# The beginning of a lightning-attention and feed-forward kernel put in another order: planner lengths, half groups of tokens, filler transposes

## The chip, the core and the metric

The kernel runs on one core of a Trainium2 chip. Such a core has a matrix engine (TensorE, here PE, with its weight loads shown as PEld), VectorE (DVE), ScalarE (ACT), GpSimd (POOL) and SyncE (SP), which here only issues transfers. The engines run side by side, each takes its own instructions strictly in the order in which the program lists them, and they wait for each other through semaphores. Matrix products land in PSUM banks; everything else lives in SBUF or in the device's memory (DRAM). The metric is the device time of one execution in microseconds; the figure for the kernel before is the median of six runs, 640.48 us (636.88 to 642.76).

## The reference

```python
batch, n_heads, seq, head_dim = (4, 8, 768, 64)      # blocks of 64 tokens
for b in range(nb):
    qb, kb, vb = (q[:, :, sl], k[:, :, sl], v[:, :, sl])
    intra = np.einsum('bhic,bhjc->bhij', qb, kb) * Dmask[None]
    intra = np.einsum('bhij,bhjd->bhid', intra, vb)
    inter = np.einsum('bhid,bhde->bhie', qb * lam_pow[None], kv_state)
    out[:, :, sl] = intra + inter
    kv_state = lam_block[None, :, None, None] * kv_state + np.einsum('bhsd,bhse->bhde', kb * rev_pow[None], vb)
...
n_tokens, d_model, d_ff = (3072, 512, 2048)
h = x @ w_in                       # x: the attention output as (3072, 512)
g = np.maximum(0.01 * h, h)
return (g @ w_out).astype(np.float32)
```

The two weight matrices arrive as 64-bit floats; the kernel converts them itself.

## The kernel before

**Chunks.** Attention works on 24 chunks of 128 tokens (two blocks of 64), six to each batch. A chunk takes five steps: `load_kq` and `load_v` (SP), `transposes` (L290: PE turns k and q around, ACT copies both out of PSUM, POOL multiplies k by its decay, and q times its decay is made by DVE in the first four chunks and by POOL later), `scores` (L324: 32 small PE products for the scores and up to 32 for the state update, then on DVE the product with the decay mask, L346, and the state additions, L351 and L353, with POOL's L356 in between), and `outputs` (L361: PE products into `po`; a tiny copy, L385, that orders the two halves; then ACT writes the rounded head `xh`, L401, DVE the remainder `xl`, L402, and a combination `xm`, L404).

**Weights.** A feed-forward product in float32 quality is made of three products of fp32r parts: high, low and a difference ("h", "l", "m"). `w_in(p)` (L490) makes the three parts of 256 columns of w_in, for p = 0 to 7: two loads of 64-bit raw words, for each of them three ACT passes (L465, L467, L469) and two DVE passes (L471, L472), then `parts` (L474): `wh` on ACT (L478) or DVE (L480), `wl` (L483) and `wm` (L485) on DVE. All eight weights go through one workspace `w32` and one scratch tile `low`.

**Units.** `up(g, p)` (L512) multiplies group g (four chunks, 512 tokens) by weight p: for each half f of the 256 columns four matmuls h and four l into one of two banks `b1`, four m into the one bank `b2`; ACT scales the former (L530), DVE adds the latter (L533), ACT applies the leaky ReLU to the pair (L536), SP stores it to DRAM. There are six groups of eight units. After all of them `down` (L561) multiplies by w_out, from about 380 us on.

**What sets the order.** Class `Plan` (L37) collects operations with an engine, a length in microseconds written at the call, the buffers read and written, and a rank. `emit` (L77) walks forward in planned time, always takes the operation that can start first (the lower rank in a tie), and emits the instructions in the order of planned starts. On the chip only that order remains: each engine runs its list and waits where its inputs are late.

**The list before.** `seq` (L588 to L605) says which operations are ranked first: the first four chunks each alone ("a"), then chunk 4 begun ("b"), after that "rounds" ("r", L424) in which one chunk's outputs, the next one's scores and the one after that's transposes run together; weights ("wi") come just before the first unit that needs them; units in the order group 0 with weights 0 to 3, group 1 with weights 0 to 3, group 0 with 4 to 7, group 1 with 4 to 7, and then group after group. Ten transposes of an identity matrix (L223) stand at the head of PE's list.

Of the kernel before, what the change touches and what calls it, by code (L numbers as in the profile page):

```python
# [36 lines left out]
class Plan:  # L37
# [6 lines left out]
    def __init__(self):  # L44
        self.ops, self.last, self.rank = [], {}, 0.0
        self.chain, self.chains = None, {}

# [9 lines left out]
    def add(self, eng, us, fn, reads=(), writes=(), rank=0.0):  # L57

        n, deps = len(self.ops), set()
        for k in reads:  # L60
            w, r = self.last.setdefault(k, [None, []])
            if w is not None:
                deps.add(w)
            r.append(n)
        for k in writes:
            w, r = self.last.setdefault(k, [None, []])
            if w is not None:
                deps.add(w)
            deps.update(r)
            self.last[k] = [n, []]  # L70
        deps.discard(n)
        ways = {eng: us} if isinstance(eng, str) else dict(zip(eng, us))
        if self.chain is not None:
            self.chains[self.chain].append(n)
        self.ops.append((ways, fn, deps, (self.rank + rank, n)))

    def emit(self):  # L77
# [14 lines left out]
        free = dict.fromkeys(("PE", "ACT", "DVE", "POOL", "DMA"), 0.0)  # L92
# [15 lines left out]
        while len(done) < n:  # L108
# [16 lines left out]
            free[e] = t + ways[e]  # L125
# [7 lines left out]
        self.timeline = sorted(done)  # L133
        for t, _, i, e in self.timeline:
            ways, fn = self.ops[i][:2]
            fn() if len(ways) == 1 else fn(e)
# [3 lines left out]
def kernel(  # L140
# [23 lines left out]
    WARM = 10  # L164
    HALF = (slice(0, D), slice(D, 2 * D))
# [22 lines left out]
    low = sb([P, d_model], "low", I32)  # L188
# [33 lines left out]
    for _ in range(WARM):  # L222
        nc.tensor.transpose(out=b2[:, 0:P], in_=ident, identity=ident)  # L223
    nc.gpsimd.memset(zero, 0.0)
    plan = Plan()
    add = plan.add
# [20 lines left out]
    add("DVE", 5.0, factors_k, [], ["fk", "sc"])  # L247
    add("DVE", 2.0, factors_q, [], ["fq"])
# [20 lines left out]
    def updates(c):  # L269

        if c < GC:
            return [(z.rearrange("p (y t) -> p y t", y=HP)[:, :, 0:D], k) for z, k in ((b1[1], "b11"), (b2, "b2"))]
        return [(psc[:, t, upper, :], "psc") for t in range(2)]
# [16 lines left out]
    def transposes(c):  # L290
        b, n, i = of(c)
        tk, tq = kqv[0][i], kqv[1][i]
        if c < GC:
            z, key = b1[0].rearrange("p (y t) -> p y t", y=HP), "b10"
            at = [z[:, y, :] for y in range(HP)]
        else:
            z, key = po[:, :, upper, :], "po"
            at = [po[:, y // 2, HP + y % 2 * 2:HP + y % 2 * 2 + 2, :].rearrange("p a t -> p (a t)") for y in range(HP)]
# [25 lines left out]
    def scores(c):  # L324
        b, n, i = of(c)
        tk, tv, kT, qT, pu = kqv[0][i], kqv[2][i], kTs[i], qTs[i], updates(c)
# [8 lines left out]
        def kv():  # L335
            for y in range(HP):
                for x in range(2):
                    for t in range(n_pu):
                        h = y // 2 + (2 * y + x) % HP * 2
                        quad(pu[t][0][:, y, :], t, tk[:, 2 * y + x, :], tv[:, h, :], x, start=y == 0)  # L340

        add("PE", 0.47, go, [f"kT{i}", f"qT{i}"], ["psc"])
        add("PE", 0.47, kv, [f"k{i}", f"v{i}"], sorted({pu[t][1] for t in range(n_pu)}))

        def uses():
            add("DVE", 0.69, lambda: nc.vector.tensor_tensor(sc, psc[:, :, lower, :], decay, op=ALU.mult), ["psc", "fk"], ["sc"])  # L346
            for t in range(n_pu):
                j = 2 * c + t
                new = state[j % 4]
                if n == 0 and t == 0:  # L350
                    add("DVE", 0.42, lambda new=new: nc.vector.tensor_copy(new, pu[0][0]), [pu[0][1]], [f"st{j % 4}"])  # L351
                else:
                    add("DVE", 0.42, lambda new=new, t=t: nc.vector.tensor_tensor(new, new, pu[t][0], op=ALU.add),  # L353
                        [pu[t][1]], [f"st{j % 4}"])
                if n_pu == 2:
                    add("POOL", 0.7, lambda new=new, j=j: nc.gpsimd.tensor_tensor(state[(j + 1) % 4], new, _bc(lam_c, 2, D), op=ALU.mult),  # L356
                        [f"st{j % 4}", "fq"], [f"st{(j + 1) % 4}"])
# [3 lines left out]
    def outputs(c, between=lambda: None):  # L361
# [38 lines left out]
        def uses():  # L400
# [4 lines left out]
                [h, l], [m])  # L405
# [37 lines left out]
    def to_float32(kind, p, h, dst, key):  # L443
# [3 lines left out]
        r = raw[j]  # L447
# [13 lines left out]
        def addend(dt, i):  # L461
# [6 lines left out]
            [f"raw{j}"], ["low"])  # L468
        add("ACT", 0.77, lambda: nc.scalar.activation(out=addend(F16, 1), in_=words(1, F32), func=AF.Copy, bias=0.0, scale=2.0 ** -100),  # L469
            [f"raw{j}"], ["low"])  # L470
        add("DVE", 0.42, lambda: nc.vector.tensor_scalar(d, d, 3, None, op0=ALU.logical_shift_left), [], [key])  # L471
        add("DVE", 1.0, lambda: nc.vector.tensor_tensor(d, d, low, op=ALU.add), ["low"], [key])  # L472

    def parts(p, src, keys):  # L474
        wh, wl, wm = W[p]
        def head(e):
# [7 lines left out]
            keys + [f"wh{p}"], [f"wl{p}"])  # L484
        add("DVE", 1.25, lambda: nc.vector.scalar_tensor_tensor(wm, wl.bitcast(F32), -1.0, wh.bitcast(F32), op0=ALU.mult, op1=ALU.add),  # L485
# [24 lines left out]
    n_t = 0  # L510

    def up(g, p):  # L512
        nonlocal n_t
        x, w = X[g % 2], W[p]
        jg = (g * NP + p) % 2

        def product(dst, f, z, start):
            for kk in range(KO):
                nc.tensor.matmul(dst, lhsT=w[z][:, kk * 2 * P + f * P:kk * 2 * P + (f + 1) * P], rhs=x[z][:, kk, :],  # L519
                                 start=start and kk == 0, stop=kk == KO - 1, skip_group_check=True)  # L520

        def keys(z):
            return [f"w{z}{p}"] + [f"x{z}{g % 2}{cc}" for cc in range(GC)]

        for f in range(2):
            jt, n_t = n_t % 2, n_t + 1
            t, r, b, kb = tt[jt], gs[jg][:, f, :], b1[jt], f"b1{jt}"
            add("PE", 0.91, lambda f=f, b=b: product(b, f, 0, True), keys("h"), [kb])
            add("PE", 0.91, lambda f=f, b=b: product(b, f, 1, False), keys("l"), [kb])
            add("ACT", 0.6, lambda t=t, b=b: nc.scalar.activation(out=t, in_=b, func=AF.Copy, bias=0.0, scale=(1.0 + 1.0 / S) / U),  # L530
                [kb], [f"t{jt}"], rank=-1.5)
            add("PE", 0.91, lambda f=f: product(b2, f, 2, True), keys("m"), ["b2"])
            add("DVE", 0.69, lambda t=t, r=r: nc.vector.scalar_tensor_tensor(r, b2, -1.0 / WS, t, op0=ALU.mult, op1=ALU.add),  # L533
                [f"t{jt}", "b2"], [f"gs{jg}"], rank=-1.5)
        y = gs[jg]
        add("ACT", 1.05, lambda: nc.scalar.activation(out=y, in_=y, func=AF.Prelu, bias=0.0, scale=1.0, alpha=0.01),  # L536
            [], [f"gs{jg}"], rank=-1.5)
        add("DMA", 1.5, lambda: nc.sync.dma_start(out=G[g][p], in_=y.rearrange("p f t -> p (f t)")), [f"gs{jg}"], [f"G{g}{p}"])
# [49 lines left out]
    steps = [(0, p) for p in range(4)] + [(1, p) for p in range(4)] + [(g, p) for g in range(2) for p in range(4, NP)]  # L588
    steps += [(g, p) for g in range(2, NG) for p in range(NP)]
    seq = [("a", c) for c in range(GC)] + [("b", GC)]  # L590
    seen = set()
    nxt, n_out = GC, 0
    for n, (g, p) in enumerate(steps):
        if p not in seen:
            seen.add(p)
            seq.append(("wi", p))
        seq.append(("up", g, p))
        over = sum((s, NP - 1) in steps[:n + 1] for s in range(NG))
        if nxt < NCH and nxt // GC < over + 2:
            seq.append(("r", nxt))  # L600
            nxt += 1
        if n >= 16 and n_out < NP and n % 2 == 0:
# [9 lines left out]
    for n, x in enumerate(seq):  # L612
# [3 lines left out]
        elif x[0] == "wi":  # L616
            plan.rank = n - 4.0
# [46 lines left out]
```

## Time and profile before

| | us |
|---|---|
| median of six runs | 640.48 |
| the profiled execution, its own time | 636.88 |
| its span, first to last instruction | 635.1 |
| PE busy | 612.0 (96%), 5450 matmuls |
| weight loads busy (beside the matmuls) | 506.4 (80%) |
| DVE busy | 358.9 (57%), 475 instructions |
| ACT busy | 274.3 (43%) |
| POOL busy | 80.9 (13%) |
| chain that ended last | PE 87%, DVE 6%, DMA 2%, ACT 2%, issue 1% |

The span lies inside the execution's time; 1.8 us are around it. The profiled execution is the fastest of the six. "Idle" of an engine is time in which it had nothing running; a row of the timeline gives its start, its length, what it does, how many instructions it merges, and in brackets the idle time before it with what ended that. PE is busy for 96% of the whole, but not evenly: the mean hides the first 80 us, where five of the page's 40 slices (15.9 us each) show PE at 7, 6, 9, 9, 7 tenths and DVE at 5, 8, 9, 9, 9.

### The profile page before, as it was taken

The numbers are of one execution on the slowest core, as the hardware profiler recorded it, in microseconds if no ns is written. First come the engines' busy times: TensorE is split into PE (matmuls) and PEld (weight loads), VectorE is DVE, ScalarE is ACT, GpSimd is POOL, SyncE is SP. The second block draws the span as 40 slices with busy tenths as digits, with TensorE's granted clock in tenths as the row PEclk, the third lists the DMA queues.
The fourth block names the chain that finished last, engine by engine and source line by source line (L and its number), as shares of the span: only waits on it lengthen the run. The fifth ranks groups of instructions, "written<-read, shape, count | busy, mean of one in ns | idle before, by whom it ended". The sixth has DMA issues, their size and how long they took to land.

```text
span 635.1 us, 13063 instructions
## 1 busy us (share of the span) xinstructions
PE 612.0 (96%) x5450; PEld 506.4 (80%) x5450; DVE 358.9 (57%) x475; ACT 274.3 (43%) x399; POOL 80.9 (13%) x91
## 2 busy tenths in 40 slices
PE   7699799998989999999999999999999999999997
PEld 6577588887878888887888888888888888888885
DVE  5899978565655344244247876463635545454531
ACT  4477678875667444443433532321312222313111
POOL 3444302032340142040000000000000000000000
PEclk9799999999999999999999999999999999999999
DMA  9868857688895554243425664342432524343201
GB/s 214 205 182 248 212 202 242 221 253 267 252 274 177 183 142 129 90 131 117 163 105 194 217 214 155 110 142 90 150 116 89 177 72 144 117 133 115 85 0 67
DMA packets 102091, 101.52 MB, mean 160 GB/s; under 512 B 78480, under 2 KB 78480, under 8 KB 102032
## 3 DMA queue, kind: packets, MB, share of 16 engines
q1 hardware_dynamic: 101888, 100.68, 50.5%
q8 instruction: 43, 0.70, 0.5%
q14 instruction: 16, 0.13, 0.1%
q10 hardware_dynamic: 144, 0.00, 0.0%
HBM read 65.02 MB, written 35.65 MB: 159 GB/s over the span
## 4 chain that ended last, share of the span: by engine, by line
PE 87%; DVE 6%; DMA 2%; ACT 2%; issue 1%; SPq 0%; ACTq 0%; DVEq 0%
PE b L519 37%; PE b L571 17%; PE po L571 10%; PE psc L571 10%; PE po L253 4%; PE pt L571 3%; PE psc L253 3%; PE pt L302 1%; PE po L302 1%; DVE wl L483 1%; DMA raw<-in_moe_w_out_dram 1%; DMA att<-in_k_dram 1%; DVE w L472 1%; DVE xl L402 1%; DVE wh L480 1%
## 5 line engine op out<-in xcount | busy, mean ns | idle before, releaser
L533 DVE SCALAR_TENSOR_TENSOR gs<-b,t 128x512 f32<-128x512 f32 x96 | 66.2, 690 | 91.2 <-PE b L519 83.0
L555 ACT ACTIVATE xh<-att 128x1024 fp32r<-128x1024 f32 x48 | 50.9, 1061 | 141.0 <-PE po L571 138.3
L556 DVE SCALAR_TENSOR_TENSOR xl<-att,xh 128x1024 fp32r<-128x1024 f32 x48 | 58.7, 1222 | 93.4 <-ACT xh L555 93.3
L519 PE MATMUL b<-xh,wh 128*128 128x512 f32 x384 | 104.9, 396 | 1.7 <-ACT xh L401 1.7
L519 PE MATMUL b<-xm,wm 128*128 128x512 f32 x384 | 103.5, 392 | 1.5 <-DVE gs L533 1.4
L519 PE MATMUL b<-xl,wl 128*128 128x512 f32 x384 | 102.9, 391 | 1.1 <-DVE xl L402 1.1
L530 ACT ACTIVATE t<-b 128x512 f32<-128x512 f32 x96 | 57.1, 595 | 85.3 <-PE b L519 83.0
L519 PEld LDWEIGHTS b<-xm,wm 128*128 128x128 f32 x384 | 71.7, 188 | 17.3 <-DVE gs L533 2.3
L519 PEld LDWEIGHTS b<-xl,wl 128*128 128x128 f32 x384 | 72.0, 188 | 16.6 <-DVE xl L402 1.5
L519 PEld LDWEIGHTS b<-xh,wh 128*128 128x128 f32 x384 | 70.6, 188 | 17.3 <-ACT xh L401 2.3
L571 PE MATMUL b<-wh,xh 128*128 128x512 f32 x192 | 74.8, 390 | 0.0
L571 PE MATMUL b<-wl,xl 128*128 128x512 f32 x192 | 74.8, 390 | 0.0
L536 ACT ACTIVATE gs<-gs 128x1024 f32<-128x1024 f32 x48 | 50.6, 1055 | 37.8 <-DVE gs L533 37.8
L558 DVE SCALAR_TENSOR_TENSOR xm<-xl,xh 128x1024 fp32r<-128x1024 f32 x48 | 58.7, 1225 | 4.6
L253 PE MATMUL po<-att 64*64 64x64 f32 x1472 | 35.3, 230 | 10.8 <-DVE att L346 4.1
L315 POOL TENSOR_TENSOR att<-att 128x512 f32<-128x512 f32 (+1 forms) x24 | 26.9, 1119 | 136.0 <-PE po L302 126.5
L253 PEld LDWEIGHTS po<-att 64*64 64x64 f32 x1472 | 29.1, 141 | 16.6 <-issue 7.9
L571 PEld LDWEIGHTS b<-wl,xl 128*128 128x128 f32 x192 | 36.1, 188 | 7.4
L571 PEld LDWEIGHTS b<-wh,xh 128*128 128x128 f32 x192 | 36.1, 188 | 7.4
L571 PE MATMUL po<-wh,xh 128*128 128x512 f32 x96 | 37.4, 390 | 0.0
L571 PE MATMUL psc<-wl,xl 128*128 128x512 f32 x96 | 37.4, 390 | 0.0
L571 PE MATMUL po<-wm,xm 128*128 128x512 f32 x96 | 37.4, 390 | 0.0
(73 smaller groups left out, 829.8 us busy)
## 6 DMA issues: line engine op xcount, KB each, us to landing
g<-gs SPq DMA_DIRECT2D x48, 512.0 KB, 3.4
att<-g SPq DMA_DIRECT2D x48, 512.0 KB, 3.3
raw<-in_moe_w_in_dram SPq DMA_DIRECT2D x16, 512.0 KB, 4.4
raw<-in_moe_w_out_dram SPq DMA_DIRECT2D x16, 512.0 KB, 4.4
att<-in_k_dram SPq DMA_DIRECT2D x48, 128.0 KB, 4.3
att<-in_q_dram SPq DMA_DIRECT2D x48, 128.0 KB, 3.7
att<-in_v_dram SPq DMA_DIRECT2D x24, 256.0 KB, 4.5
out_dram<-gs SPq DMA_DIRECT2D x24, 256.0 KB, 2.1
```

The costliest lines, as they stand in the source:

```text
L253: nc.tensor.matmul(dst[HALF[cols]], lhsT=lhsT[HALF[rows]], rhs=rhs[HALF[rows]], start=start, stop=True, skip_group_check=True)
L302: nc.tensor.transpose(out=at[y], in_=src[:, 2 * y:2 * y + 2, :].rearrange("p a d -> p (a d)"), identity=ident)
L315: add("POOL", 1.15, lambda: nc.gpsimd.tensor_tensor(kr[nr], kr[nr], _bc(pow_k, 3, D)[nr], op=ALU.mult), ["fk"], [f"k{i}"])
L402: add("DVE", 0.7, lambda: nc.vector.tensor_tensor(tok(xl), y, tok(xh.bitcast(F32)), op=ALU.subtract), ["po", h], [l])
L519: nc.tensor.matmul(dst, lhsT=w[z][:, kk * 2 * P + f * P:kk * 2 * P + (f + 1) * P], rhs=x[z][:, kk, :], start=start and kk == 0, stop=kk == ...
L530: add("ACT", 0.6, lambda t=t, b=b: nc.scalar.activation(out=t, in_=b, func=AF.Copy, bias=0.0, scale=(1.0 + 1.0 / S) / U), [kb], [f"t{jt}"] ...
L533: add("DVE", 0.69, lambda t=t, r=r: nc.vector.scalar_tensor_tensor(r, b2, -1.0 / WS, t, op0=ALU.mult, op1=ALU.add), [f"t{jt}", "b2"], [f"g ...
L536: add("ACT", 1.05, lambda: nc.scalar.activation(out=y, in_=y, func=AF.Prelu, bias=0.0, scale=1.0, alpha=0.01), [], [f"gs{jg}"], rank=-1.5)
L555: add("ACT", 1.05, lambda: nc.scalar.activation(out=h, in_=graw[j], func=AF.Copy, bias=0.0, scale=NEAR), reads, wr("h"))
L556: add("DVE", 1.25, lambda: nc.vector.scalar_tensor_tensor(l, graw[j], 1.0, h.bitcast(F32), op0=ALU.mult, op1=ALU.subtract), reads + [f"rh{ ...
L558: add("DVE", 1.25, lambda: nc.vector.scalar_tensor_tensor(m, l.bitcast(F32), -S, h.bitcast(F32), op0=ALU.mult, op1=ALU.add), [f"rh{j}", f" ...
L571: nc.tensor.matmul(acc[tb][z // 2], lhsT=ring[j][z][:, f * T + tb * P:f * T + (tb + 1) * P], rhs=W[pp][z][:, f * d_model:(f + 1) * d_model ...
```

## The change

- **Planner.** `free` starts DVE at 3.5 us and the transfers at 1.3 us; a PE operation before 20 us of planned time counts 1.5 times its length; a DVE operation counts longer while POOL is planned busy (0.4 of the overlap). The lengths of the decay factors become 2.0 and 1.9 us (5.0 and 2.0 before).
- **Fillers.** When PE is planned idle for over 0.4 us, `emit` puts transposes of the identity (0.22 us each) into PE's list ahead of the next operation, until the first unit writes bank `b10`. The ten at the head stay, so the first k transposes stand behind 29 of them; in all there are 51 instead of 10.
- **Half groups.** `up(g, p, half)` multiplies 256 tokens by weight p: 24 matmuls of 128x256, both halves f in one bank, so that one ACT scaling, one DVE addition, one shorter leaky ReLU and one store serve them. Four units are split in two so: (0,0), (0,1), (1,1), (0,7). That is 192 matmuls of 256 columns in place of 96 of 512.
- **Order.** A list written out for the first two groups; weights in the order 0, 1, 2, 3, 4, 5, 7, 6. The first unit, a half one, needs two chunks instead of four.
- **Banks and buffers.** The first chunks' state updates go to `psc` (before: `b11` and `b2`) and precede the scores; their k transposes go to `b11` (before: `b10`); `low` has two copies; `xm` of the first four chunks has a later rank; weights lose their rank bonus of four places.

```diff
+        free = {"PE": 0.0, "ACT": 0.0, "DVE": 3.5, "POOL": 0.0, "DMA": 1.3}
...
-            free[e] = t + ways[e]
+            us = ways[e]
+            if e == "PE" and t < self.cold:
+                us *= 1.5
+            elif e == "DVE" and fn is not None and free["POOL"] > t:
+                us += 0.4 * min(free["POOL"] - t, us)
+            free[e] = t + us
...
+            if e == "PE":
+                if self.spare in self.ops[i][4]:
+                    self.idle = None
+                if self.idle is not None and t > last + 0.4:
+                    self.idle(int((t - last - 0.2) / 0.22))
+                last = t + ways[e]
...
+    def busy(n):
+        for _ in range(n):
+            nc.tensor.transpose(out=b1[0][:, 0:P], in_=ident, identity=ident)
+    busy(WARM)
...
+    plan.idle, plan.spare = busy, "b10"
...
+    pu = [psc[:, t, upper, :] for t in range(2)]
...
+        add("PE", 0.47, kv, [f"k{i}", f"v{i}"], ["psc"])
         add("PE", 0.47, go, [f"kT{i}", f"qT{i}"], ["psc"])
-        add("PE", 0.47, kv, [f"k{i}", f"v{i}"], sorted({pu[t][1] for t in range(n_pu)}))
...
-                [h, l], [m])
+                [h, l], [m], rank=LATER if c < GC else 0.0)
...
-    def up(g, p):
+    def up(g, p, half=None):
+        toks = slice(0, T) if half is None else slice(half * T // 2, (half + 1) * T // 2)
+        us = 0.91 if half is None else 0.49
...
+            return [f"w{z}{p}"] + [f"x{z}{g % 2}{cc}" for cc in range(toks.start // C, toks.stop // C)]
...
+    seq = [("a", 0), ("wi", 0), ("a", 1), ("a", 2), ("up", 0, 0, 0), ("a", 3), ("wi", 1), ("up", 0, 1, 0), ("b", 4),
+           ("wi", 2), ("up", 0, 0, 1), ("up", 0, 1, 1), ("r", 4), ("r", 5), ("r", 6), ("up", 0, 2), ("r", 7), ("wi", 3),
+           ("up", 0, 3), ("wi", 4), ("up", 1, 1, 0), ("up", 0, 4), ("wi", 5), ("up", 1, 2), ("up", 1, 4), ("up", 0, 5),
+           ("wi", 7), ("up", 1, 7), ("up", 0, 7, 0), ("wi", 6), ("up", 0, 7, 1), ("up", 0, 6), ("up", 1, 3), ("r", 8),
+           ("r", 9), ("r", 10), ("r", 11), ("up", 1, 6), ("up", 1, 1, 1), ("up", 1, 5), ("up", 1, 0)]
```

## The prediction

> **What bounds the kernel now.** I first read busy time by stage, then PE's timeline in the first two stages, then DVE's rows for the same time. Columns of the first view: stretch, its length, then busy time (and instructions) of PE, PEld, DVE, ACT, POOL, the granted clock, the DMA share and GB/s.
>
> ```profile
> 0.00:34.20 34.20, 23.68 (x546) 19.19 (x546) 23.76 (x50) 15.80 (x29) 12.84 (x21) 0.90 0.86 206
> 34.20:78.07 43.87, 40.13 (x689) 31.98 (x689) 42.01 (x56) 31.73 (x53) 19.55 (x18) 1.00 0.79 220
> 78.07:160.00 81.93, 79.79 (x930) 67.16 (x931) 54.75 (x86) 60.42 (x95) 15.61 (x17) 1.00 0.73 233
> ```
>
> After 78.07 us PE is busy for 79.79 of 81.93 us, and from there to the end it is short of work by 2% or less: nothing but fewer or cheaper matmuls shortens that. Before 34.20 PE idles 10.5 us, up to 78.07 another 3.7, and there DVE is the full one (42.01 of 43.87). So the start is set by DVE, the rest by PE. PE's rows show where:
>
> ```profile
> 1.36 2.39 PE L223 MATMUL b<-att 128*128 128x128 f32 x10 [1.36 <-POOL att L224]
> 4.03 1.27 PE L302 MATMUL b<-att 128*128 128x128 f32 x4 [0.27 <-DMA att<-in_k_dram]
> 9.24 1.11 PE L302 MATMUL b<-att 128*128 128x128 f32 x4
> 16.57 0.66 PE L302 MATMUL b<-att 128*128 128x128 f32 x4
> 25.66 1.56 PE L253 MATMUL po<-att 64*64 64x64 f32 x48 [4.12 <-DVE att L346]
> ```
>
> ```profile
> 34.20 1.20 PE L519 MATMUL b<-xh,wh 128*128 128x512 f32 x4 [0.72 <-ACT xh L401]
> 65.91 1.20 PE L519 MATMUL b<-xm,wm 128*128 128x512 f32 x4 [1.39 <-DVE gs L533]
> 78.07 1.20 PE L519 MATMUL b<-xl,wl 128*128 128x512 f32 x4 [1.12 <-DVE xl L402]
> ```
>
> The first matmul of a unit starts at 34.20 us. The same four transposes take 1.11 us at 9.24 and 0.66 us at 16.57, so the array runs slowly at first; 48 small products take 1.56 us after the 4.12 us gap, 0.93 later: the gap made it slow again.
>
> Warm prices come from a round without waits:
>
> ```profile
> 97.24 0.60 PE L302 MATMUL po<-att 128*128 128x128 f32 x4
> 97.68 0.60 PE L302 MATMUL pt<-att 128*128 128x128 f32 x4
> 98.21 0.93 PE L253 MATMUL po<-att 64*64 64x64 f32 x48
> 98.96 1.11 PE L253 MATMUL psc<-att 64*64 64x64 f32 x64
> 99.89 0.41 PE L253 MATMUL po<-att 64*64 64x64 f32 x16
> 100.23 1.20 PE L519 MATMUL b<-xm,wm 128*128 128x512 f32 x4
> ```
>
> From starts: transposes of a chunk 0.97 us, scores 0.93, a whole round 2.99; a product of four matmuls 0.907 (83.64 to 84.55 and on), 0.227 each.
>
> **Lost time, before.** By 78.07, the last start that waited for DVE in this stage, PE had done 26 products (23.6 us), the outputs of 8 chunks, the scores of 9 and the transposes of 10 (8 x 2.99 + 0.93 + 2 x 0.97 = 26.8). That is 50.4 us of warm work in 78.07 us: 27.7 us were lost to idling, slow clock and start. The change can only work on these.
>
> **DVE after, walked along its new list.** I take the built programs' instruction order and the mean durations of the first 150 us, which contain their share of disturbance:
>
> ```profile
> L472 DVE CUSTOM_DVE_ANT_0 w<-w,low 128x1024 uint16<-128x1024 uint16 x23 | 18.7, 813 | 2.4 <-ACT low L469 2.1
> L471 DVE TENSOR_SCALAR w<-w 128x512 int32<-128x512 int32 x24 | 14.4, 601 | 1.3 <-ACT w L465 1.3
> L483 DVE SCALAR_TENSOR_TENSOR wl<-wh,w 128x1024 fp32r<-128x1024 f32 x8 | 11.3, 1417 | 0.6 <-ACT wh L478 0.5
> L485 DVE SCALAR_TENSOR_TENSOR wm<-wl,wh 128x1024 fp32r<-128x1024 f32 x8 | 10.8, 1346 | 0.2
> ```
>
> with gs, L346, xl, q's product 0.69 each, xm 0.735, state additions 0.41, the tiny copy 0.15. Check on before: L320 of chunk 0 at 7.49 plus the sum up to chunk 7's xl (62.8 us) plus DVE's listed idle (8.1 us) gives 78.4; the trace has 78.02.
>
> 1. Fillers, first 29: ten took 2.39 us, so at the slow clock 6.4 to 6.9 us from 1.36: they end near 8.0, where k was turned from 4.03 on. Then k transposes 1.1, two fillers 0.45, q transposes 1.1, two fillers 0.45, the 16 state products, now ahead of the scores (a small product shows as two records, so this is an x32 row), 1.08, and 16 scores 1.08: the first L346 at 13.3 instead of 8.52. That is one end. The other: the fillers make the array fast by 6.5 us, the rest of them and these steps run at the 0.66 and 0.69 us of the fast rows, and POOL's decay of k (1.06) comes last: 10.0. The trace is unclear between them: PE does little but transposes from 1.36 to 6.64 and is still slow at 9.24; it is fast from about 13, when ordinary products had come in since 7.32. That leans to the slow end, and I take 12.2. Nothing covers the delay, since DVE, past its factors at 7.4, has no other input.
> 2. From there to weight 0 finished (wm): 9.4 us of DVE work plus 0.4 waiting for POOL's state product: 22.0 us. Before, it was finished at 25.0.
> 3. From there to weight 1 finished: L346 and state of chunks 1 to 3, xl and xm of chunks 1 and 2, the products for q, weight 1 and one gs sum to 15.3 us: 37.3 us; chunk 1's xl ends on the way at 26.3, so the first unit starts near 26. ACT has 9.2 us of work for the first 8.8 of these and its raw words land near 23, so it follows just in time: no further wait, though without spare.
> 4. PE, with chunks 1 to 3 and 10 half products done while DVE worked, then runs 12 half products (12 x 0.48), 8 transposes (0.9) and chunk 4's scores and state products (0.9) to the first product of unit (0,2): 37.3 + 7.6 = 44.9 us. By then its warm work is 22 half products, 22 x 0.4535 = 10.0, and chunks 4 x 2.99 + 0.93 + 2 x 0.97 = 14.8: 24.8. Lost: 20.1 us. Gain over before: 27.7 - 20.1 = 7.6.
> 5. From there PE sets the time, if the weights keep ahead. The same DVE sum puts wl of weights 2, 3, 4, 5, 7, 6 at 44.8, 55.5, 69.0, 81.5, 90.2, 98.3; PE, adding its products and rounds, reaches them at 45.8, 58, 72.6, 88, 94, 105. Slack 1.0, 2.5, 3.6, 6.5, 4, 7 us: thin at first. Each m product also waits for the one bank b2, whose gs may stand behind a wl or wm: bounds 0 and the 3.74 us idle of before's second stage. I take 1.5, nearer the lower end, since DVE now has slack.
>
> **Half matmuls.** No row shows 128x256. From below, half of 0.227: 0.1135 us. From above, its weight load as the page times it, 0.188. Nearest row: transposes of 128 columns, each with its own load, start every 0.11 us, so a load can hide; I take 0.12. The first 96 are inside the walk; the other 96 cost 96 x 0.0065 = 0.6 us (bounds 0 and 7.2). Splitting adds no DVE or scaling work (one per half unit in place of one per f); the extra leaky ReLU and stores go to ACT and SP, off the path after 45 us.
>
> **Filler and clock.** If the fillers make the array fast, 2.2 us come off the sum (10.0 for 12.2); if they do nothing for it, 1.1 are added. Their help in the later gaps is booked at nothing, since DVE sets the pace there until 37 us. The Trainium skill, "TensorE: Matmul & The Clock Gate", section "Part 4: PE-mode transpose", speaks against the change here: transposes, it says, do not count as activity for the clock as other matmuls do. By it the start is the 13.3 of step 1 and the span 1.1 more than my sum.
>
> The other edits together (two `low`, state banks, later xm, shorter planned factors) only permit the order walked above: nothing by themselves. The two "issue" waits of PE after 80 us (3.6 us in all, the longer one, 2.14 us at 149, while w_out's raw words are late) may go or double; taken as kept, bounds +-3.6.
>
> **Sum.** 635.1 - 7.6 + 1.5 + 0.6 = 629.6 us of span, 5.5 less. The profiled execution took 636.88, but the median of the runs is 640.48; I take 5.5 off the median: 635.0 us.
>
> **Rivals.**
> - Still faster: the fillers make the array fast (2.2 off) and gs never holds PE (1.5 off): 631.3. For it: PE would be busy without a gap from 1.36 on, which it was not before; against it: the slow row at 9.24, and step 3 has no spare. Chance 0.15.
> - Lockstep, no change: five weights are made while PE depends on gs, and each long wl or wm holds one gs as at 65.91 (1.39 us): 5 x 1.39 = 7 in place of 1.5, near 640.5. For it: b2 is one bank and DVE is still 94% full there (59 us of work in 63); against it: DVE reaches each weight with slack. Chance 0.14.
> - Slower: the 256-column matmuls run at the pace of their weight loads. Without its half products my gain is 7.6 + 0.6 - 1.5 = 6.7; all 192 at 0.188 cost 192 x 0.0745 = 14.3: 640.5 - 6.7 + 14.3 = 648. It decides from 0.148 us per matmul (6.7/192 above 0.1135). For it: PEld's mean of 0.188 on all fp32r loads; against it: the transposes at 0.11. Chance 0.14.
> - That the replan does not move the real waits at all would end as the lockstep case and is inside it.
>
> The forecast holds 0.57. Less than 0.5% (3.2 us) cannot be told from no change here. Of the forecast 0.05 fall short of that, so faster is 0.52 + 0.15 = 0.67; same 0.05 + 0.13 = 0.18; slower 0.15 with the unlucky end of the lockstep. The forecast's own range is 632 to 639 (start +-2, stalls 0 to 3.7, halves); taking in most of lockstep and of the fast case: 629 to 641.
>
> **What would show it.** First matmul of a unit near 26 us instead of 34.2; first L346 near 12; wm of weight 1 done near 37; PE without waits over 1 us from 45 us on; four 256-column matmuls in 0.48 us. It would be wrong if those four take 0.75 us, if wm of weight 1 comes after 42 us, or if PE's waits for gs between 45 and 105 us sum to more than 5 us.

## The result and the profile after

| | before | after |
|---|---|---|
| median of the runs, us | 639.67 (635.13 to 644.83, 77 runs) | 634.85 (630.17 to 639.61, 35 runs) |
| the profiled execution, us | 636.88 | 635.64 |
| its span, us | 635.1 | 633.9 |
| matmuls of PE in the profile | 5450 | 5587 |
| PE's waits put down to "issue", us | 3.6 | 4.8 |

The ratio of after to before is 0.9926, with a 95% interval of 0.9912 to 0.9940: 4.7 us less, between 3.8 and 5.6. Here and below a ratio leaves out runs more than 1.5% above the fastest of the same kernel (two of the six with whole units, and one of the six in the last experiment, which took 3475 us), while a median counts all runs. The two profiled executions differ by only 1.2 us, because that of before lies 2.8 us under its kernel's median; so a balance of the two traces shows less than the runs do.

The first view of after is busy time by stage; columns as in the prediction: stretch, its length, busy time (and instructions) of PE, PEld, DVE, ACT, POOL, the granted clock, the DMA share and GB/s.

```profile
0.00:34.20 34.20, 28.61 (x610) 24.15 (x614) 25.25 (x54) 20.42 (x33) 12.29 (x19) 1.00 0.92 228
34.20:78.07 43.87, 42.29 (x757) 37.06 (x758) 37.17 (x56) 34.24 (x57) 19.39 (x19) 1.00 0.81 219
78.07:160.00 81.93, 78.37 (x843) 66.09 (x842) 49.65 (x84) 57.66 (x92) 13.48 (x15) 0.98 0.72 229
```

PE is busy for 28.61 us of the first stretch instead of 23.68 (a part of that is filler), and for 42.29 instead of 40.13 of the second, where DVE has come down from 42.01 to 37.17. In the third stretch it is the other way: PE idles 3.56 us instead of 2.14, though no input is late there for long.

The second view is PE's timeline, with start, length, operation, number of merged instructions, and the idle time before it.

```profile
1.36 5.20 PE L241 MATMUL b<-att 128*128 128x128 f32 x29 [1.36 <-POOL att L244]
6.40 0.60 PE L319 MATMUL b<-att 128*128 128x128 f32 x4
...
24.28 0.74 PE L544 MATMUL b<-xh,wh 128*128 128x256 f32 x4 [0.19 <-ACT xh L418]
...
42.21 0.64 PE L544 MATMUL b<-xl,wl 128*128 128x256 f32 x4
42.69 0.64 PE L544 MATMUL b<-xm,wm 128*128 128x256 f32 x4
43.17 0.64 PE L544 MATMUL b<-xl,wl 128*128 128x256 f32 x4
...
44.72 1.20 PE L544 MATMUL b<-xh,wh 128*128 128x512 f32 x4
```

The first k transposes, at 6.40, take the 0.60 us of a fast array; before, the same four took 1.27 at 4.03. The first product of a unit starts at 24.28 instead of 34.20. Products of four 256-column matmuls start every 0.48 us, 0.12 for each matmul. The first product of unit (0,2) starts at 44.72.

The third view is DVE's timeline: the first decay-mask product (L363 here, L346 before) and the last parts of weights 0 and 1.

```profile
9.43 0.69 DVE L363 TENSOR_TENSOR att<-psc,att 128x512 f32<-128x512 f32 x1 [0.70 <-PE psc L274]
18.45 1.22 DVE L506 SCALAR_TENSOR_TENSOR wm<-wl,wh 128x1024 fp32r<-128x1024 f32 x1
34.20 1.22 DVE L506 SCALAR_TENSOR_TENSOR wm<-wl,wh 128x1024 fp32r<-128x1024 f32 x1
```

Weight 0 is finished at 19.7 us, weight 1 at 35.4. What PE waited for, in the whole run (total, times, longest):

```profile
PE po L274 <- issue: 4.8, 2, 2.7
PE b L319 <- DMA att<-in_k_dram: 2.2, 3, 0.8
...
PE b L544 <- DVE gs L569: 0.7, 2, 0.4
PE b L544 <- DVE wl L500: 0.5, 1, 0.5
```

DVE hardly holds PE any longer: 0.7 us for `gs` in all. The greatest wait is one for nothing that this view knows, and it comes late (what it is for stands in the last section):

```profile
142.00 0.28 PE L274 MATMUL po<-att 64*64 64x64 f32 x3
144.93 0.61 PE L274 MATMUL po<-att 64*64 64x64 f32 x13 [2.66 <-issue]
145.47 2.07 PE L544 MATMUL b<-xh,wh 128*128 128x512 f32 x4
147.35 1.62 PE L544 MATMUL b<-xl,wl 128*128 128x512 f32 x4
148.80 1.09 PE L544 MATMUL b<-xm,wm 128*128 128x512 f32 x4
```

In the middle of sixteen small products PE stops for 2.66 us, with its inputs there; and the array is slow afterwards: from start to start the two products behind it last 1.88 and 1.45 us instead of 0.907, 1.5 us more. The granted clock of this trace is 0.50 from 145.1 to 148.5 us.

**Where the gain went.** I counted lost time in both traces as the prediction does (start of an instruction, less the warm work before it: 0.227 us for a matmul of 512 columns, 0.1134 for 256, 0.11 for a transpose of the program's own, 0.0156 for a record of a small product, nothing for a filler). The prices are rounded, so a difference between the two kernels is good to some 0.5 us.

| lost up to | before, us | after, us | gain, us |
|---|---|---|---|
| 78 us (before: the wait at 78.07 taken in) | 29.4 | 23.8 | 5.6 |
| 140 us | 30.2 | 27.0 | 3.2 |
| 200 us | 37.0 | 35.9 | 1.1 |
| 378 us | 41.0 | 39.6 | 1.4 |

The beginning gives 5.6 us. Some 2.4 go by 140 us: two short waits (0.5 for ACT, 0.4 for `gs`), the later half units at 0.12 instead of 0.1134 per matmul (0.5), the rest spread in pieces too small for the count. Another 2 go between 140 and 200 us, where PE stops for 2.66 and 2.12 us instead of 2.14 and 1.49 and is slow after the first. This is one execution of each; the runs, which average over such stops, say 4.7.

### The profile page after: what moved, and what is told of

Its sections match the earlier page's. It is cut to its first block, busy times and chain, and to the rows that moved or that the text cites. A ratio compares the mean times of both kernels' runs of the same rounds, so it can differ in the third digit from the quotient of the medians.

```text
span 633.9 us, 13360 instructions
## 1 busy us (share of the span) xinstructions
PE 615.9 (97%) x5587; PEld 514.6 (81%) x5587; DVE 350.1 (55%) x475; ACT 277.3 (44%) x403; POOL 79.4 (13%) x91
## 4 chain that ended last, share of the span: by engine, by line
PE 86%; DMA 6%; ACT 2%; issue 2%; SPq 2%; DVE 1%; ACTq 0%; DVEq 0%
PE b L544 36%; PE b L607 17%; PE po L607 10%; PE psc L607 10%; PE po L274 4%; PE pt L607 3%; PE psc L274 3%; DMA raw<-in_moe_w_in_dram 3%; DMA raw<-in_moe_w_out_dram 2%; PE po L319 1%; SPq L299 1%; PE pt L319 1%; DMA att<-in_k_dram 1%; DMA att<-in_v_dram 1%; ACT gs L571 1%
## 5 line engine op out<-in xcount | busy, mean ns | idle before, releaser
L544 PE MATMUL b<-xh,wh 128*128 128x512 f32 (+1 forms) x416 | 107.7, 381 | 0.8 <-ACT t L565 0.5
L544 PE MATMUL b<-xl,wl 128*128 128x512 f32 (+1 forms) x416 | 105.6, 376 | 0.5 <-DVE wl L500 0.5
L544 PE MATMUL b<-xm,wm 128*128 128x512 f32 (+1 forms) x416 | 104.8, 376 | 0.7 <-DVE gs L569 0.7
L544 PEld LDWEIGHTS b<-xl,wl 128*128 128x128 f32 x416 | 75.3, 190 | 14.9 <-DVE wl L500 0.7
L544 PEld LDWEIGHTS b<-xh,wh 128*128 128x128 f32 x416 | 74.3, 190 | 15.9 <-ACT t L565 1.1
L544 PEld LDWEIGHTS b<-xm,wm 128*128 128x128 f32 x416 | 73.8, 188 | 15.4 <-DVE gs L569 1.5
L571 ACT ACTIVATE gs<-gs 128x1024 f32<-128x1024 f32 (+1 forms) x52 | 51.5, 991 | 40.8 <-DVE gs L569 40.5
L607 PE MATMUL pt<-wm,xm 128*128 128x512 f32 x96 | 37.4, 390 | 0.0
L607 PE MATMUL po<-wm,xm 128*128 128x512 f32 x96 | 37.4, 390 | 0.0
L607 PE MATMUL po<-wl,xl 128*128 128x512 f32 x96 | 37.4, 390 | 0.0
L607 PE MATMUL psc<-wh,xh 128*128 128x512 f32 x96 | 37.4, 390 | 0.0
```

The costliest lines, as they stand in the source:

```text
L571: add("ACT", 1.05 if half is None else 0.6, lambda: nc.scalar.activation(out=y, in_=y, func=AF.Prelu, bias=0.0, scale=1.0, alpha=0.01), [] ...
L607: nc.tensor.matmul(acc[tb][z // 2], lhsT=ring[j][z][:, f * T + tb * P:f * T + (tb + 1) * P], rhs=W[pp][z][:, f * d_model:(f + 1) * d_model ...
```

## The experiments

All are edits of the changed kernel unless said otherwise, and each ratio is to the kernel before on the same chip.

**The changed kernel again, unchanged.**

> The changed kernel once more, unchanged, as the yardstick of this call. If the trace of after is typical: first score product on DVE (L363) at 9.4 us, first unit matmul at 24.3, weight 1 finished at 35.4, first product of unit (0,2) at 44.7, all within 0.5 us. Two mid-run stops of PE in the small products of a round (2.7 and 2.1 us in after, 2.1 and 1.5 in before, no semaphore behind them): if they belong to the program they come back at the same instructions with the same length; if they belong to the execution, place or length changes and with it the time. Time 4 to 6 us under before.

635.68 us, ratio 0.9939 (0.9914 to 0.9965); span 634.3. The beginning repeats itself (first L363 at 9.93, first unit at 24.38, weight 1 at 35.4). The stops come at the same two places (2.41 us at 145.81, 1.30 at 183.56), and a third one, 1.18 us at 35.22, is new. So their places recur, their lengths do not.

**No fillers.**

```diff
-    plan.idle, plan.spare = busy, "b10"
+    plan.idle, plan.spare = None, "b10"
```

> The 41 planned filler transposes left out, the ten at the head kept, nothing else changed. Theory A (the recorded forecast: fillers are mostly delay while DVE sets the pace): first L363 near 8.5 instead of 9.4, weight 1 finished 0 to 1 us earlier, time equal or up to 2 us less than the changed kernel. Theory B (the fillers make the array fast, as the 0.60 us transposes at 6.4 suggest): k transposes back at 1.1 us each four, L363 at 8.5 to 9.5 all the same, slow rows until 13 and again after a gap near 18 to 21, weight 1 finished 1 to 2 us later, time 1 to 3 us more than the changed kernel.

633.77 us, ratio 0.9903 (0.9871 to 0.9936); span 630.1. PE's timeline of this kernel:

```profile
1.36 2.39 PE L241 MATMUL b<-att 128*128 128x128 f32 x10 [1.36 <-POOL att L244]
4.00 1.24 PE L319 MATMUL b<-att 128*128 128x128 f32 x4 [0.25 <-DMA att<-in_k_dram]
...
6.79 1.98 PE L274 MATMUL psc<-att 64*64 64x64 f32 x64 [0.35 <-DMA att<-in_v_dram]
...
11.70 1.11 PE L319 MATMUL b<-att 128*128 128x128 f32 x4 [0.56 <-DMA att<-in_k_dram]
...
20.21 0.93 PE L274 MATMUL po<-att 64*64 64x64 f32 x48 [0.74 <-DVE att L363]
...
24.71 1.03 PE L544 MATMUL b<-xh,wh 128*128 128x256 f32 x4 [1.41 <-ACT xh L418]
```

The array is slow until about 18 us: 1.98 us at 6.79 for the 64 records that took 1.16 at 8.20 with fillers, 1.11 us for four transposes at 11.70. Yet the k transposes begin 2.4 us sooner, and the two cancel: first L363 at 8.84, first unit at 24.71 (24.28 with fillers), weight 1 at 35.8 (35.4). The fillers do warm the array, and the warmth pays for the wait behind them and no more. The two late stops are gone in this kernel; the only one is 1.76 us at 58.53.

**Whole units.** The four split units are put back as whole ones, at the place of their second halves; the rest of the list stays.

```diff
-    seq = [("a", 0), ("wi", 0), ("a", 1), ("a", 2), ("up", 0, 0, 0), ("a", 3), ("wi", 1), ("up", 0, 1, 0), ("b", 4),
-           ("wi", 2), ("up", 0, 0, 1), ("up", 0, 1, 1), ("r", 4), ...
+    seq = [("a", 0), ("wi", 0), ("a", 1), ("a", 2), ("a", 3), ("wi", 1), ("b", 4),
+           ("wi", 2), ("up", 0, 0), ("up", 0, 1), ("r", 4), ...
```

> The four split units put back together (each where its second half stood), rest kept; fillers are planned anew for the longer wait. If the half groups are what fills PE early: the first unit starts only after chunk 3, near 36 us instead of 24.3, PE idles about 11 half products (5 us) more before 45 us and the time rises by 3 to 5 us. If PE would have caught up anyway behind DVE's weights: under 1 us more, or less by the 1.2 us that 192 matmuls of 256 columns cost over 96 of 512 (0.12 against 0.1135 each).

651.16 us over all six runs (642.16 to 654.61), ratio 1.0128 (1.0063 to 1.0192) over four of them; span 647.1, far worse than expected. The first unit in PE's timeline, and the second stage of this kernel:

```profile
36.53 3.53 PE L544 MATMUL b<-xh,wh 128*128 128x512 f32 x8 [2.95 <-ACT xh L418]
```

```profile
34.20:78.07 43.87, 39.29 (x556) 32.85 (x557) 29.73 (x47) 31.41 (x51) 17.04 (x16) 0.92 0.71 189
```

The first product waits for all four chunks, until 36.53 us, and after 2.95 us of idling the array is slow: eight matmuls take 3.53 us. In the next stage PE is busy 39.29 us and DVE only 29.73: neither is full. PE also stops more often, 7.3 us in all, and `gs` costs 2.4. Lost time by the count above: 26.3 us at 45, 31.6 at 78, 37.4 at 105, 52.3 at 378. So this list needs the halves: without them it loses all its gain and some 8 us more (4 to 12). Whole units with a list made for them were not tried.

**The planner's old lengths.** Start times, the factor for the cold array, the overlap with POOL and the lengths of the decay factors as before; list, halves and fillers stay (23 transposes at the head).

```diff
-        free = {"PE": 0.0, "ACT": 0.0, "DVE": 3.5, "POOL": 0.0, "DMA": 1.3}
+        free = dict.fromkeys(("PE", "ACT", "DVE", "POOL", "DMA"), 0.0)
...
-            if e == "PE" and t < self.cold:
-                us *= 1.5
-            elif e == "DVE" and fn is not None and free["POOL"] > t:
-                us += 0.4 * min(free["POOL"] - t, us)
...
-    add("DVE", 2.0, factors_k, [], ["fk", "sc"])
-    add("DVE", 1.9, factors_q, [], ["fq"])
+    add("DVE", 5.0, factors_k, [], ["fk", "sc"])
+    add("DVE", 2.0, factors_q, [], ["fq"])
```

> The planner's start times, slow-clock factor, POOL factor and factor lengths as before; list, halves, banks and filler rule kept (fewer fillers are planned at the head, about 13 of the 19). If measured lengths matter: some instruction comes too early in an in-order queue and blocks, weight 1 finished 1 to 3 us later, time 1 to 3 us more than the changed kernel. If the list alone decides the order: within 1 us of it, or a little less because of the shorter head.

636.92 us, ratio 0.9947 (0.9927 to 0.9967); span 635.6. The start is the same (first unit 24.58, weight 1 at 35.9). PE's waits differ:

```profile
PE b L540 <- DVE gs L565: 3.6, 4, 1.3
PE b L315 <- DMA att<-in_k_dram: 2.5, 2, 2.3
```

The wait for `gs` grows from 0.7 to 3.6 us, and lost time at 105 us from 24.7 to 30.9; between 45 and 105 us DVE is busy for 56.67 us instead of 50.69. The longest stop of this execution is 0.4 us instead of 2.66 and 2.12, which offsets part of that. In time the intervals of this kernel and the changed one overlap; the effect of the lengths is not resolved.

**List and halves alone:** no fillers and the old lengths, that is, the edits of the second and fourth experiment together.

> The changed kernel without fillers and with the planner lengths of before: what is left is the written list, the half groups and the banks. If these carry the gain: 4 to 7 us under before, within 1.5 us of the changed kernel. If measured lengths and fillers carry part of it together: 2 us or more above the changed kernel.

635.01 us, ratio 0.9941 (0.9913 to 0.9969); span 632.4; first unit 24.86, weight 1 at 36.8. With the new list, the halves and the banks alone (and the two `low` and the later `xm`, which stayed in) the kernel is as fast as the changed one, within the intervals. Together they carry the gain; fillers and lengths add nothing that these runs can show. What the banks, the two `low` and the later `xm` bring was not tried apart from the list.

**Stops and the count of instructions.** The changed kernel stops at the same two places in both its profiles, and without fillers both stops are gone: do they follow the number of instructions that PE has run? I replaced the head of PE's list with another number of instructions. The first try, without fillers:

```diff
-    WARM = 10
+    WARM = 6
+    SHIFT = 32
...
+    for _ in range(SHIFT):
+        nc.tensor.matmul(b2[0:D, 0:D], lhsT=ident[0:D, 0:D], rhs=ident[0:D, 0:D], start=True, stop=True, skip_group_check=True)
...
-    plan.idle, plan.spare = busy, "b10"
+    plan.idle, plan.spare = None, "b10"
```

> The kernel without fillers, its head of ten transposes replaced by six and by 32 products of 64x64 (about 120 more instructions on PE, about the same time), everything after it in the same order. Theory F (PE's instructions arrive in blocks of 256, and a block used up inside one round of small products is not followed in time): the stop of 1.8 us that the run without fillers had in a round at 58.5 us is gone or elsewhere, every stop left stands within 20 instructions of a multiple of 256 counted anew, time changed by up to 3 us either way although no dependence changed. Rival G (the stop is a late transfer or semaphore that the profile does not show): the stop stays in the same round at 58.5 us with 1.5 to 2 us.

638.04 us, ratio 0.9987 (0.9960 to 1.0014); span 638.1. My head was far dearer than meant:

```profile
2.83 7.09 PE L246 MATMUL b<-att 64*64 64x64 f32 x64
9.85 1.11 PE L322 MATMUL b<-att 128*128 128x128 f32 x4
...
143.64 0.33 PE L277 MATMUL po<-att 64*64 64x64 f32 x3 [2.38 <-issue]
```

All 32 products use one quarter of the array and follow each other at 0.22 us (7.09 for 32); so the k transposes start 5.85 us late and the first unit at 29.79, 5.1 after that of the kernel without fillers. The stop at 58.53 is gone, others have come: 2.38 us at 143.64, 0.39 at 150.68, 2.27 at 187.47. Counted from the first instruction they are not within 20 of a multiple of 256, as theory F said, but 89, 91 and 96 short of one; the last section comes back to this. The spans of the two kernels differ by 8.0 us, and these two things add up to 8.4: 5.1 of start, and 5.04 us of stops instead of 1.76. The ratios differ by 0.0084, or 5.4 us.

The same head in the kernel before (ten transposes replaced there):

> The kernel before with the same shift by about 120 instructions at its head and nothing else changed. Theory F: the stops of 2.1 us at 150.6 and 1.5 us at 187.7 leave their places; if no new ones come, the time falls by 3 to 4 us, more than half of what the whole change brought. Rival G: both stops stay at the same instructions and the time stays within 1 us of before.

639.58 us, ratio 1.0018 (0.9990 to 1.0047). Its stops of 2.14 and 1.49 us are gone; new ones are 0.73 at 61.52, 1.28 at 69.64 and 1.17 at 182.08. The fall by 3 to 4 us that theory F allowed for did not come. The first unit starts 5 us later (39.25), and the time is the same to within 3 us (the upper end of the interval). So there at least part of the delay is covered: what set the time of the kernel before came after its first unit.

The changed kernel with `WARM = 0` in place of 10, so that 19 fillers stand at the head instead of 29:

> The changed kernel without the ten transposes at the head: 19 planned ones remain, ending near 4.7 to 5 us instead of 6.4 (PE still warmed). Theory A: L363 1 to 1.5 us earlier (near 8.2), weight 1 finished up to 1 us earlier, time 0 to 2 us less than the changed kernel. Theory B (warmth is what counts): array not yet fast at the first k transposes, nothing gained. Theory F adds: 20 instructions fewer, so the stops near 145 and 183 us move by 20 instructions and may shrink.

635.35 us, ratio 0.9944 (0.9918 to 0.9970). The first four k transposes take 1.06 us at 5.46, those of q 0.60 at 6.65: the array becomes fast between them, as theory B had it. First L363 at 8.96, first unit at 24.82, weight 1 at 35.7: a shorter head frees nothing. The stops are 2.59 at 144.36 and 1.84 at 188.57.

Then a head that costs little: two transposes, and 32 small products that change from quarter to quarter of the array.

```diff
-    WARM = 10
+    WARM = 2
...
+    def small(n):
+        for i in range(n):
+            r, c = HALF[i // 2 % 2], HALF[i % 2]
+            nc.tensor.matmul(po[c, i // 2 % 2, 0, :], lhsT=ident[r, 0:D], rhs=ident[r, 0:D], start=True, stop=True, skip_group_check=True)
+    small(32)
```

In the kernel before:

> The kernel before, its head of ten transposes replaced by two and by 32 small products that use the four quarters of the array in turn, as the kernel's own do: about 112 instructions more on PE, but this time the first k transposes should start within 0.6 us of 4.0, so only the place of the 256-instruction blocks moves. Theory F: no stop at the ends of the rounds at 150.6 and 187.7; new ones at other places, again at whole multiples of 256, shorter (0.7 to 1.3 us as in the first shifted run of this kernel); time 1 to 4 us under before. Rival H (the stops merely moved and cost as much elsewhere): within 1 us of before.

637.29 us, ratio 0.9982 (0.9959 to 1.0006). Again both stops of before are gone, and others are there: 1.09 at 13.57, 1.29 at 182.35, 0.62 at 248.22. In time the interval leaves room for theory F and for rival H.

In the changed kernel without fillers:

> The same shift in the kernel without fillers, as a clean repeat of the first shifted run, whose head was 5.9 us late by mistake (first k transposes at 9.85). Theory F: the stops of that run come back, at the same instructions (in the rounds near 139 and 182 us now, 2.4 and 2.3 us), the one at 58.5 stays away; time 2 to 4 us above the run without fillers. If the start delay of that run was what cost it 4.3 us: time back within 1 us of the run without fillers, stops or not.

631.72 us, ratio 0.9904 (0.9866 to 0.9942); span 629.1. First L368 at 8.25, first unit at 24.57. The four stops are 0.77, 0.96, 0.71 and 1.19 us, not the 2.4 and 2.3 of the sixth experiment, though three of them fall on the same counts as there: the place was foretold, the length was not. The time is that of the kernel without fillers (0.9904 and 0.9903), as the last sentence of the expectation had it, with 3.63 us of stops for 1.76. The sixth experiment, whose k transposes start 5.8 us later than here, stands at 0.9987, and the intervals do not meet: in the changed kernel, without its fillers at least, a late start costs time.

In the changed kernel with its later fillers, 40 small products and three transposes at the head:

```diff
-    plan.idle, plan.spare = busy, "b10"
+    first = [True]
+    def fill(n):
+        if first[0]:
+            first[0] = False
+            small(40)
+            n = 3
+        busy(n)
+    plan.idle, plan.spare = fill, "b10"
```

> The changed kernel with its head of 29 transposes replaced by 40 such small products and three transposes (about 108 instructions more, head over near 4.3 us instead of 6.4), later fillers kept. Theory F: the stops at 144.9 and 183.4 (2.7 and 2.1 us, with a slow array after the first) go or shrink; with k turned 2 us earlier the time falls 2 to 5 us under the changed kernel, the best of the study. If the blocks land badly: stops of the same sum at other places, time within 1 us of the changed kernel.

631.77 us over all six runs, 631.04 over the five that the ratio counts, 0.9895 (0.9854 to 0.9936); span 629.3. No stop above 0.3 us is left. The round that held the longest one of the changed kernel, in PE's timeline here:

```profile
143.35 1.11 PE L286 MATMUL psc<-att 64*64 64x64 f32 x64
144.29 0.41 PE L286 MATMUL po<-att 64*64 64x64 f32 x16
144.63 1.20 PE L556 MATMUL b<-xh,wh 128*128 128x512 f32 x4
145.66 1.07 PE L556 MATMUL b<-xl,wl 128*128 128x512 f32 x4
```

No stop within the small products, and the products behind run at full pace (1.03 and 0.91 us from start to start). Lost time at 378 us is 35.0 us instead of 39.6. This is the lowest ratio of the study, but its interval overlaps that of the changed kernel, so a gain over it is not shown.

## Why the prediction was right

The forecast, 635.0 us, stands beside a median of 634.85, and the likeliest case is the one that came: an earlier first unit, and PE setting the time from 45 us on. That the two figures meet so closely is luck: the gain was 4.7 us for 5.5, and the median of before, from which the 5.5 were taken off, came down from 640.48 to 639.67 with more runs. The mechanism holds; two sizes did not, and they made up for each other: the start (step 1) and the stretch from weight 1 to unit (0,2) (step 4).

- **Step 1, fillers and start.** Mis-sized. I took 12.2 us for the first L363, between 10.0 with a fast array and 13.3 with a slow one, leaning to slow because PE was still slow at 9.24 in the trace before. It came at 9.43 (9.93 in the second profile): the fillers make the array fast, 29 of them taking 5.20 us instead of the 6.4 to 6.9 of the slow clock (one every 0.213 us up to the 18th, one every 0.109 us from the 19th on, at 5.1 us), and what follows runs at the fast rows' prices. The Trainium skill, "TensorE: Matmul & The Clock Gate", section "Part 4: PE-mode transpose", by which transposes don't count as activity, is not borne out here: nothing but transposes ran from 1.36 to 6.40, and the four behind them took 0.60 us, where ten transposes and a gap left four at 1.24 (second experiment). What misled me was the trace of before, where ten fillers were too few.
- **"3.7" of delay.** By the sum, the start stood 3.7 us later than before (12.2 for 8.52). It was 0.9 later; and without fillers it is 8.84, still 0.3 later than before, since there the state products precede the scores in any case.
- **Steps 2 and 3, weights 0 and 1.** Finished at 19.7 (22.0 taken) and 35.4 (37.3): early by the 2 to 2.8 us of step 1, the walk along DVE's list itself good to about 1 us. First unit at 24.28 for "near 26".
- **Step 4, (0,2) at 44.9.** 44.72, though 2.8 us of head start had come in at step 1, and 1.9 were left at the end of weight 1. Mis-sized the other way: from there to (0,2) PE takes 9.3 us for the 7.6 of the sum. The work is the same (12 half products, eight transposes, chunk 4's small products); but PE waits twice (0.17 us for `xh`, 0.48 for `xl`), and the half products behind transposes or small products last 0.56 to 0.64 us from start to start instead of 0.48. PE, busy for 8.65 of these 9.30 us, is the full one by then, and DVE (7.37) no longer is. Lost 20.1 by the sum, 20.7 by the count.
- **Step 5, 1.5 us of stalls.** `gs` cost 0.7 us in all, and no weight was waited for after 33.4 us. Not on my list was a wait of 0.92 us for k at 54.54, whose transfer comes late. Lost time still grows by 3.1 us from 44.72 to 78, more than the 1.5 set aside for `gs`; beside the wait for k it is spread over rounds and half products in small pieces. By the same count before lost 29.4, where the prediction had 27.7, so the gain at 78 us came out as forecast (5.6 for 5.5).
- **Half matmuls.** 0.12 us, as taken; the rival that put them at 0.188 is out.
- **The old "issue" waits, taken as kept.** Here the sum was 2.7 us too low for this execution: 4.8 us in place of 3.6, and 1.5 of slow array behind. The bound of ±3.6 held it. That the longer one belonged to late raw words of w_out, which I had set beside it, is not borne out: PE waits there for a block of its own instructions (below).
- **What else was not in the sum.** Of 5.6 us of gain at 78 us some 2.4 were gone by 140 us, in the one execution of each that was profiled; the runs give 4.7 for the 5.5 forecast.
- **The other edits, booked at nothing.** Measured lengths: 0.9939 against 0.9947 with fillers, 0.9903 against 0.9941 without; that is 0.5 and 2.4 us with intervals that overlap, so no effect is shown. Fillers: nothing or a small loss. The list with the halves carries the change (0.9941 alone), and this list does not do without the halves (1.0128).
- **Rivals.** Lockstep did not come: `gs` never held PE for over 0.42 us, and DVE, which the rival put at 94% there, was busy for 50.69 us (84%) of the 60 from 45 to 105. With the old lengths the waits for `gs` sum to 3.6 us, but only one, of 0.96 us at 90.45, has its `gs` behind a `wl`. "Still faster" had its first condition met, a fast array, and nearly the second (0.7 us for `gs`), and its 631.3 us still did not come: of what the fast array saved at 9 us, 0.2 us was left at 44.72, where PE sets the time, and stops and small waits took more later on.

## What to carry to other kernels

Price a new start through to the engine that is full later: here the start came 2.8 us sooner than forecast at 9 us, and 0.2 us of that was left at 45. The hand-made order and the size of its pieces were one change here: with the pieces put back whole, the same order lost more than it had gained. And where an engine stops without a semaphore, count its instructions up to the stop in several kernels, and look at the packets of the instruction queue, before looking for late data.

## What the runs showed of the hardware

**Stops of PE at fixed counts of instructions.** PE stops with no late input, mostly in the midst of small products. The stage view, from 0 to just within such a stop, counts what PE and PEld have run until then. After, without 10 of the fillers, without fillers but with the cheap head, and before, in this order, one stop each:

```profile
0.00:143.60 143.60, 134.21 (x2130) 114.98 (x2131) 105.38 (x179) 102.53 (x166) 42.67 (x50) 1.00 0.81 231
```

```profile
0.00:143.07 143.07, 133.52 (x2130) 114.64 (x2131) 104.57 (x179) 102.63 (x166) 43.20 (x50) 1.00 0.81 232
```

```profile
0.00:142.60 142.60, 132.23 (x2130) 111.85 (x2131) 103.96 (x177) 102.62 (x166) 43.47 (x50) 0.98 0.81 231
```

```profile
0.00:149.50 149.50, 134.17 (x2002) 110.27 (x2002) 115.75 (x182) 101.18 (x164) 44.13 (x50) 0.98 0.77 222
```

Three kernels that differ in the instructions at the head and in the later fillers stop after exactly 2130 matmuls and 2131 weight loads, 4261 in all; before stops 257 earlier, at 4004. All 31 stops of 0.39 us or more in the 13 profiles, by kernel (the sum of both counts):

```
before                4004  5276
changed kernel        4261  5280
the same again        1205  4261  5280
no fillers            1967
whole units           1205  1967  3752  4006  4771  6808
old lengths           4262
list and halves       1968
no fillers, long head 4007  4261  5280
before, long head     1966  2220  5022
19 fillers            4261  5534
before, small head     445  5022  6805
no fillers, small h.  1205  4007  4261  5280
40 small products     none
```

The same few numbers recur, and the steps between them are whole multiples of about 254 or 255 (3752 to 4006: 254; 4261 to 5280: 4 x 255; 4261 to 5534: 5 x 255). All 31 counts are 67 to 107 short of a multiple of 256, the later ones by more. This fits a border every 256, if the view leaves out some 65 instructions ahead of the first and one or two per block. The page counts something of this kind too:

```profile
q8 instruction: 44, 0.72, 0.5%
```

44 packets of 16 KB with 5587 matmuls and as many loads (11174/256 = 43.6), and 43 packets with 5450 (42.6). So PE's instructions come in blocks of 256 by a transfer, and it stops when the next block isn't there. The packets of queue q8 in the traces bear this out. The 2.66 us stop of after runs from 142.28 to 144.93 us; its packet starts at 142.71 and takes 0.95 us, and PE goes on 1.27 us after its end. In all 31 stops PE goes on 1.20 to 1.59 us after the end of a q8 packet, in a queue whose packets are 3 to 30 us apart in after; and it is always the same packet: at the stop that stands at n times 256 by the reckoning above (17 times for 4261) it is packet n - 1 of that execution. A late packet of instructions is thus what PE waits for, not a late input. Not every border has a stop: the blocks ahead of a stop in before, after and the kernel without fillers were used up in 2.4 to 4.6 us (the stop left out), most others in 5 to 28; but blocks of 3.6 us passed without a stop too. Why a packet comes late, and by how much (stops of 0.4 to 2.7 us, other in each execution), stays open, as does the price in time: the three profiles with the lowest spans (629.1, 629.3 and 630.1) have 3.7, 0.3 and 2.0 us of stops, and their ratios overlap that of the changed kernel.

**Transposes make the array fast.** 29 fillers in a row do, and 19 with the four transposes behind them (fast from 6.5 us on); ten with pauses behind them don't, as shown above. The clock column doesn't show this slowness. The stage view of before has, for its first 13 us, a granted clock of 1.00 (third figure from the end), while the four transposes of 9.24 take 1.11 us:

```profile
0.00:13.00 13.00, 10.57 (x156) 8.38 (x159) 6.26 (x22) 3.89 (x7) 3.48 (x11) 1.00 0.86 209
```

The clock records of each trace begin only where the array is first fast: at 5.1 us after, at 13.5 before, at 18.1 without fillers. Time without a record counts as full clock in the column. From the first record on it does show the slow array: 0.50 from 23.8 to 30.6 us in before.

**Small products in one quarter of the array.** 0.22 us each, when all use the same quarter (7.09 us for 32, on an array still slow: the four transposes behind take 1.11 us); with the quarters changing, 64 records take 1.11 us on a fast array and 1.98 on a slow one, 0.03 and 0.06 for a product. The 32 products of one quarter also all write the same place; which of the two holds them up was not separated.
